# Loading k and q of the first two head pairs in long runs, with a repriced plan, in an attention and two-layer expert kernel

## The chip, the cores and the metric

One core of one Trainium2 chip runs the whole program. The metric is device time in microseconds of one execution, the median of several runs.

## The reference

Three layers, all in float32 (cut to what is computed):

```python
scores = 30 * tanh(q @ k.T / sqrt(64) / 30)      # 4 batches x 12 heads, 448 x 448, head size 64
x = softmax(scores) @ v                          # joined to 1792 tokens x 768
h = ((x @ w1) * (x @ w2)) @ w3 @ w_out           # 768 -> 1024 -> 1024 -> 768
e = argmax(h @ w_gate + modality_bias[modality_id]); gate = softmax(...)[e]
out[token] = gate * (relu(h @ m1[e]) @ m2[e])    # 8 experts
```

The weights w1, w2, w3 and w_out arrive as 64-bit floats and are brought to 32 bits on the chip.

## The kernel before

**Stages.** The attention stage handles 24 pairs of heads one after the other and, beside them, converts the 64-bit weights (in pieces: `L289` loads a piece into `raw`, four or five operations at `L224` to `L244` narrow it) and folds w3 with w_out into one matrix (`L648` to `L650`). Then `phase_x12` multiplies batches 0 and 1 of x with w1 and w2, `phase_x2` with the folded matrix, both again for batches 2 and 3, and at the end come the expert tiles. In these products each number is split into a high and a low part of type float32r, and a product is three passes: high weight by high x (`L1000`), high weight by low x (`L1001`), low weight by high x (`L1002`).

**A pair in the attention stage.** `load_k` (`L437`) and `load_q` (`L441`) bring both heads of a pair into `k2` and `q2`, with the order position group, head, element in each partition: the two heads of one position group lie side by side, so the load moves runs of 64 elements, 256 bytes. `load_v` (`L447`) brings v on POOL's queue. `tr_k` and `tr_q` turn k and q on TensorE (`L460`, `L474`) into a bank of the kind `tr`, of which there are two; `k_out` and `q_out` copy them out as KT and QT (`L252` on ScalarE or `L254` on VectorE). Scores are made at `L487`, tanh and exp at `L492` to `L498` into tiles of the kind `th` (seven buffers), sums of the exps on VectorE (`L523` to `L527`) and TensorE (`L534`, copied out as `smt`), and pv at `L507`. At the beginning 30 transposes of the identity (`L750`) keep TensorE busy; they hold one of the two `tr` banks until the last is done.

**The order of the work** in the attention stage is not written by hand. The class `Schedule` holds tasks with an engine, a duration in ns, a key (about four per pair), dependencies, and buffers that they take and use. `run` picks, again and again, the task that can start first, the smaller key first among equals, and emits it; so each engine's queue has the order of the plan. A load has a price `dma` in ns, which the plan adds to one common transfer queue: the load is taken to land when that queue has reached it, plus 1,100 ns. A dependency written `(lk, 0)` counts from the issue of the load and not from its landing. The plan alone decides order; on the chip an instruction waits for the tiles that it reads and overwrites. After the plan's end the stages are emitted in program order.

**At the seam**, x of batch 0 is split at `L933` (high parts, ScalarE) and `L935` (low parts, VectorE) in three pieces of two of its six 128-row blocks.

Of the kernel before, what the change touches and what calls it, by code (L numbers as in the profile page):

```python
# [8 lines left out]
F32 = mybir.dt.float32  # L9
# [111 lines left out]
def attention_moe_moe_kernel(  # L121
# [37 lines left out]
    nc = tc.nc  # L159
    B, H, S, D = q.shape  # L160
# [3 lines left out]
    P = 128  # L164
    CP = 112
    NC = S // CP
    KD = DM // P
# [32 lines left out]
    at1 = tc.alloc_tile_pool(name="at1", bufs=2, side="right", reuse_waits="tile")  # L200
# [6 lines left out]
    mm = nc.tensor.matmul  # L207
# [55 lines left out]
    class Stream:  # L263
# [17 lines left out]
        def add(self, pieces):  # L281
            n = len(pieces)
            self.todo += [(p, i, n) for i, p in enumerate(pieces)]
# [128 lines left out]
    sel = at1.tile([P, D], F32, name="sel", tag="sel", bufs=1)  # L412
    nc.gpsimd.memset(sel, 1.0)

    raw_qkv = {}

    def rows_of(r):
        return slice(D * r, D * r + D)
# [5 lines left out]
    def keys(t, g):  # L424

        return t[:, 4 * D:S].rearrange("h (p c) d -> h p c d", c=3) if g else t[:, 0:4 * D].rearrange("h (p c) d -> h p c d", c=4)

    def heads(t, p):
        b, hp = divmod(p, H // 2)
        return t[b, 2 * hp:2 * hp + 2]  # L430

    def load_k(p):
        k2 = at2.tile([P, NC, 2, D], F32, name="k2", tag="k2")
        q2 = at2.tile([CP, NC, 2, D], F32, name="q2", tag="q2")
        raw_qkv[p] = (k2, q2)
        for g in range(2):
            nc.sync.dma_start(k2[rows_of(g), 0:NC - g], keys(heads(k, p), g).rearrange("h p c d -> p c h d"))  # L437

    def load_q(p):
        eng = nc.sync if p else nc.scalar  # L440
        eng.dma_start(raw_qkv[p][1], heads(q, p).rearrange("h (p c) d -> p c h d", c=NC))  # L441

    def load_v(p):
        vt[p] = at1.tile([P, NC + NB, D], F32, name="vt", tag="vt", bufs=NV)
# [297 lines left out]
    add = sch.add  # L742

    def do(fn, *args):
        return lambda: fn(*args)
# [3 lines left out]
    for c in range(30):  # L749
        add("PE", 175, 1e6, lambda: nc.tensor.transpose(warm[:, 0:P], ident, ident),  # L750
            take=[("tr", "warm")] if c == 0 else [], use=[("tr", "warm")])
# [28 lines left out]
    for c in range(NW):  # L780
        u = c // 2
        key = (4.0 * c + 3) if c < 8 else (10 + 10.0 * c)
        raw, y, un = ("wraw", c), ("y", c), ("unit", u)
# [8 lines left out]
        if c < 8:  # L792
# [3 lines left out]
            for j in range(2):  # L796
                x = add("PE", 320, kg, do(tr_wo, c, j), [cn3[-1], *gate[-1:], *cps[-1:]], take=[tt[j], *([] if j else [("th", "o", c)])], use=[tt[j], y, ("th", "o", c)])
# [23 lines left out]
    for p in range(NP + 1):  # L821
        raw, vk, kt, qt = ("raw", p), ("v", p), ("KT", p), ("QT", p)
        hk, hq, sk, pk = ("tr", "k", p), ("tr", "q", p), ("sums", p), ("pv", p - 1)
        dep, use, take = [], [], []
        if p:
            dep, take, use = [ex[3], lv], [pk], [pk, ("th3", p - 1), ("v", p - 1)]
        if p < NP:
            k0, kk = 4 * p - 7, 4 * p - 4.0
            lk = add("SP", 1260, k0, do(load_k, p), take=[raw], use=[raw], dma=640)
            lq = add("SP" if p else "ACT", 630, k0 + 0.1, do(load_q, p), [(lk, 0)] if p else [], use=[raw], dma=640)  # L830
            lv = add("POOL", 2800, k0 + 4.0, do(load_v, p), [(lk, 0)], take=[vk], use=[vk], dma=640)
            t = add("PE", 380, 4 * p - 5.2, do(tr_k, p), [lk], take=[hk], use=[hk, raw])
            kl = add({'DVE': (620, 0), 'ACT': (530, 300)}, 0, kk, lambda eng, p=p: k_out(p, eng), [t], take=[kt], use=[hk, kt])
            t = add("PE", 380, 4 * p - 5.2, do(tr_q, p), [lq], take=[hq], use=[hq, raw])
            last_at2.append(t)
            ql = add({'DVE': (620, 0), 'ACT': (530, 300)}, 0, kk, lambda eng, p=p: q_out(p, eng), [t], take=[qt], use=[hq, qt])
            dep, take, use = dep + [kl, ql], take + [("sc", p, 3)], use + [("sc", p, 3), kt, qt]
        joint = add("PE", 770, 4 * p, do(pv_score, p), dep, take=take, use=use, mode="tiles")
        if p:

            for c in range(3):
                vl[p - 1, c] = add("PE", 770, 4 * p + c + 2.4, do(pv, p - 1, c), [ex[c], joint, vl.get((p - 1, c - 1))],
                                   use=[pk, ("th", p - 1, c), ("v", p - 1)], mode="tiles")
            smk = ("sc", "s", p - 1)
            sm = add("PE", 770, 4 * p + 2.9, do(sum_mm, p - 1), [ad], take=[smk], use=[smk, ("sums", p - 1)], mode="tiles")
            t = add({'ACT': (910, 0), 'DVE': (1090, 0)}, 0, 4 * p - 1, lambda eng, p=p: sum_out(p - 1, eng), [sm], take=[("smt", p - 1)], use=[smk, ("smt", p - 1)])
            ss = add("SP", 1260, 4 * p, do(sum_store, p - 1), [t], use=[("smt", p - 1)], dma=25)
            t = add("ACT", 530, 4 * p - 2, do(pv_copy, p - 1), [vl[p - 1, 2]], take=[("pvs", p - 1)], use=[pk, ("pvs", p - 1)])
            po[p - 1] = add("DVE", 620, 4 * p - 2, do(pv_out, p - 1), [t], use=[pk, ("pvs", p - 1)])
            st[p - 1] = add("SP", 630, 4 * p, do(pair_store, p - 1), [po[p - 1]], use=[("pvs", p - 1)], dma=640)  # L850
            last_at1 += [sm, ss] if p > NP - 2 else []
            b, r = divmod(p - 1, H // 2)
            if r == H // 2 - 1 and b < B - 1:
                t = add("SP", 630, 4 * p, lambda b=b: rs_t.__setitem__(b, sums_in(b)), [ss], dma=100)
                t = add("DVE", 500, 4 * p, lambda b=b: sums_add(rs_t[b]), [t])
                last_at2.append(add("SP", 630, 4 * p, lambda b=b: sums_out(b, rs_t[b]), [t], dma=100))
        if p == NP:
            break
        ex, ad = {}, None
        for n, c in enumerate(ORD):  # L860
            sc, th, i = ("sc", p, c), ("th3" if c == 3 else "th", p) + (() if c == 3 else (c,)), 4 * p + n
            if c < 3:
                t = add("PE", 770, i, do(score, p, c), [joint], take=[sc], use=[sc, kt, qt], mode="tiles")
            else:
                t = joint
            t = add("ACT", 600 if c == 3 else 950, i + 0.2, do(p_tanh, p, c), [t, cap_in], take=[th], use=[sc, th])
            ex[c] = add("ACT", 580 if c == 3 else 950, i + 1.1, do(p_exp, p, c), [t], use=[th])
        for c in (1, 2, 3):
            ad = add("DVE", 660 if c == 3 else 1120, 4 * p + 0, do(psum, p, c), [ex[c], *([ex[0]] if c == 1 else []), ad],
                     take=[sk] if c == 1 else [], use=[sk, ("th3", p) if c == 3 else ("th", p, c), *([("th", p, 0)] if c == 1 else [])])  # L870
# [24 lines left out]
    for n, (f, g) in enumerate(SWEEP):  # L895
        key = 5.4 * (n + 2) + 3
        raw, r_, h_, w_ = ("w3raw", n), ("w3r", n), ("tr", "w", n), ("w3t", n)
# [10 lines left out]
        for half in range(2):  # L908
# [3 lines left out]
                       take=[] if half else [fo], use=[fo, w_, ("unit", 2 * g), ("unit", 2 * g + 1)])  # L912
# [75 lines left out]
    def phase_x12(half, bs, hooks):  # L988
        gt = gp.tile([P, 2, KF, HALF], F32R, name="gT", tag="gT")
        units = {}  # L990
        for i, (u, j) in enumerate(ORDER[half]):
            if u not in units:
                units[u] = (ws.take(), ws.take())
            x = xt[bs[j]]
            for w, (wh, wl) in enumerate(units[u]):
                acc = acc2()
                for ft in range(2):
                    for d in range(KD):
                        o = d * 256 + ft * P
                        mm(acc[:, ft, :S], lhsT=wh[:, o:o + P], rhs=x[:, 0, d, :], start=(d == 0), stop=False)  # L1000
                        mm(acc[:, ft, :S], lhsT=wh[:, o:o + P], rhs=x[:, 1, d, :], start=False, stop=False)  # L1001
                        mm(acc[:, ft, :S], lhsT=wl[:, o:o + P], rhs=x[:, 0, d, :], start=False, stop=(d == KD - 1))  # L1002
                if w == 0:
                    a = wide("a").rearrange("p (f s) -> p f s", f=2)
                    nc.scalar.copy(a, acc[:, :, :S])
                else:
                    nc.vector.tensor_tensor(out=a, in0=acc[:, :, :S], in1=a, op=ALU.mult)
                    fs, sl = slice(2 * u, 2 * u + 2), slice(j * S, j * S + S)
                    nc.vector.tensor_copy(gt[:, 0, fs, sl], a)  # L1009
                    nc.gpsimd.tensor_tensor(out=gt[:, 1, fs, sl], in0=a, in1=gt[:, 0, fs, sl], op=ALU.subtract)  # L1010
                if u in [v for v, _ in ORDER[half][:i]]:
                    ws.free()
                ws.tick(nc.scalar, nc.vector)
                if (i, w) in hooks:
                    hooks[i, w]()
        return gt
# [332 lines left out]
```

## Time and profile before

| what | value |
|---|---|
| runs shown | 958.78, 961.33, 965.59 us; median 961.33 |
| the profiled execution | 963.59 us, span 961.7 us, mean granted TensorE clock 0.989 |
| TensorE busy | 924.1 us of the span |
| VectorE, ScalarE, POOL busy | 469.1, 374.9, 241.0 us |
| transfers | 132.73 MB, 138 GB/s over the span |

The span runs from the first to the last instruction. PE is TensorE and PEld its weight loads, DVE is VectorE, ACT is ScalarE; SPq and ACTq are the queues on which SyncE and ScalarE issue transfers. [...] Busy matmuls overlap, so a busy TensorE can still be slower than it could be.

### The profile page before, as it was taken

What the parts mean: (1) busy time and instruction counts of PE and PEld (TensorE: products, weight loads), DVE (VectorE), ACT (ScalarE), POOL (GpSimd) and SP (SyncE); (2) the same over time, 40 slices, a digit from 0 to 9 for tenths busy, and PEclk for the clock granted to TensorE, in tenths of its full rate; (3) what the DMA queues carried; (4) which work ended last, traced back from release to release, by engine and by line L of the source; (5) the groups of instructions that cost most, each with busy time, mean ns of one, the idle gap of its engine ahead of it and who ended that gap; (6) DMA issues with size and microseconds to landing.
All of it is one profiled execution on the core that took longest, in us unless ns stands there. A gap on an engine that the chain in (4) does not pass through costs nothing. (4 is left out here: it accounts for less than half of the span.)

```text
span 961.7 us, 13900 instructions
## 1 busy us (share of the span) xinstructions
PE 924.1 (96%) x5618; PEld 763.5 (79%) x5618; DVE 469.1 (49%) x671; ACT 374.9 (39%) x447; POOL 241.0 (25%) x211
## 2 busy tenths in 40 slices
PE   8999989999999999999999999999999999999994
PEld 5456555655655799999999999999899899889894
DVE  4999986786675478721006422100653523423410
ACT  4897766776775333231222211211422312322400
POOL 3434211151110112123542441200604212302011
PEclk9899999999999999999999999999999999999998
DMA  9767785477544565626622341310671591782401
GB/s 225 206 167 219 203 243 141 129 217 179 156 140 121 146 193 164 186 79 215 171 93 96 78 120 34 115 50 33 166 178 43 184 172 33 199 148 52 160 20 44
DMA packets 126088, 132.73 MB, mean 138 GB/s; under 512 B 60926, under 2 KB 107416, under 8 KB 126021
## 3 DMA queue, kind: packets, MB, share of 16 engines
q1 hardware_dynamic: 112644, 114.35, 42.3%
q0 software_dynamic: 12464, 17.22, 7.9%
q8 instruction: 46, 0.75, 0.3%
q10 hardware_dynamic: 912, 0.23, 0.1%
q14 instruction: 22, 0.17, 0.1%
HBM read 102.13 MB, written 30.19 MB: 138 GB/s over the span
## 5 line engine op out<-in xcount | busy, mean ns | idle before, releaser
L1001 PE MATMUL acc<-xT,wh 128*128 128x448 f32 x384 | 141.4, 368 | 0.7 <-DVE xT L935 0.7
L1000 PE MATMUL acc<-xT,wh 128*128 128x448 f32 x384 | 140.4, 366 | 1.5 <-ACT xT L933 1.5
L1002 PE MATMUL acc<-xT,wl 128*128 128x448 f32 x384 | 140.4, 366 | 0.0
L329 DVE TENSOR_TENSOR wl<-raw,wh 128x1536 fp32r<-128x1536 f32 (+1 forms) x42 | 73.6, 1759 | 116.8 <-ACT wh L252 116.8
L252 ACT CAST wh<-raw 128x1536 fp32r<-128x1536 f32 (+1 forms) x48 | 70.3, 1479 | 105.4 <-DMA raw<-in_moe_w_dram 78.5
L487 PE MATMUL sc<-QT,KT 64*64 64x448 f32 x672 | 92.9, 561 | 7.9 <-ACT smt L252 4.2
L507 PE MATMUL pv<-th,vt 64*64 64x448 f32 x672 | 89.2, 551 | 0.0
L498 ACT ACTIVATE th<-th,capb 128x448 f32<-128x448 f32 (+1 forms) x96 | 89.0, 956 | 0.6
L1214 PE MATMUL acc<-wh,hT 128*124 128x384 f32 x256 | 87.8, 343 | 1.1 <-DVE y L1222 0.7
L447 POOL DMA_DIRECT2D vt<-in_v_dram x96 | 50.9, 545 | 146.3 <-PE pv L507 144.9
L1216 PE MATMUL acc<-wh,hT 128*124 128x384 f32 x256 | 86.5, 338 | 0.7 <-DVE hT L1185 0.7
L1215 PE MATMUL acc<-wl,hT 128*124 128x384 f32 x256 | 86.3, 337 | 0.5 <-DVE wl L329 0.5
L1010 POOL TENSOR_TENSOR gT<-a,gT 128x896 fp32r<-128x896 f32 x16 | 43.8, 2740 | 144.2 <-DVE gT L1009 138.7
L1000 PEld LDWEIGHTS acc<-xT,wh 128*128 128x128 f32 x384 | 72.5, 189 | 8.2 <-ACT xT L933 2.3
L1001 PEld LDWEIGHTS acc<-xT,wh 128*128 128x128 f32 x384 | 72.6, 189 | 7.0 <-DVE xT L935 1.2
L492 ACT ACTIVATE th<-sc,icap 128x896 f32<-128x896 f32 x72 | 71.2, 1010 | 16.2 <-PE sc L487 15.6
L1002 PEld LDWEIGHTS acc<-xT,wl 128*128 128x128 f32 x384 | 72.6, 189 | 5.3
L1032 PE MATMUL acc<-wh,gT 128*128 128x388 f32 x224 | 76.4, 341 | 0.0
L1033 PE MATMUL acc<-wl,gT 128*128 128x388 f32 x224 | 76.0, 339 | 0.0
L1034 PE MATMUL acc<-wh,gT 128*128 128x388 f32 x224 | 75.9, 339 | 0.0
L1180 PE MATMUL acc<-xsT,wh 128*128 128x496 f32 x192 | 74.9, 390 | 0.0
L1182 PE MATMUL acc<-xsT,wl 128*128 128x496 f32 x192 | 74.5, 388 | 0.0
(163 smaller groups left out, 1630.1 us busy)
## 6 DMA issues: line engine op xcount, KB each, us to landing
raw<-in_moe_w_dram SPq DMA_DIRECT2D x48, 768.0 KB
w3raw<-in_moe_w_dram SPq DMA_DIRECT2D x16, 512.0 KB
raw<-w_scr SPq DMA_DIRECT2D x8, 776.0 KB
raw<-in_moe_w_out_dram SPq DMA_DIRECT2D x8, 768.0 KB
w_scr<-y SPq DMA_DIRECT2D x16, 384.0 KB
raw<-w_scr SPq DMA_DIRECT2D x8, 768.0 KB
x_scr<-pvs SPq DMA_DIRECT2D x24, 224.0 KB
xraw<-x_scr SPq DMA_DIRECT2D x4, 1344.0 KB
```

The lines of the kernel that those rows point to most:

```text
L487: mm(sc[rows_of(side(p, j, g)), g, :S], lhsT=KT[p][rows_of(j), o:o + D], rhs=QT[p][rows_of(j), :], start=True, stop=True)
L498: nc.scalar.activation(tht[p, c], tht[p, c], ACTF.Exp, scale=capb)
L507: mm(pvb[p][rows_of(j), r, :S], lhsT=vt[p][rows_of(r), NC * g + c, :], rhs=tht[p, c][rows_of(r), g, :] if c < NB else tht[p, c][rows_of(r) ...
L1000: mm(acc[:, ft, :S], lhsT=wh[:, o:o + P], rhs=x[:, 0, d, :], start=(d == 0), stop=False)
L1001: mm(acc[:, ft, :S], lhsT=wh[:, o:o + P], rhs=x[:, 1, d, :], start=False, stop=False)
L1002: mm(acc[:, ft, :S], lhsT=wl[:, o:o + P], rhs=x[:, 0, d, :], start=False, stop=(d == KD - 1))
L1032: mm(acc[:, hf, :HA], lhsT=gt[:, 0, f, ts], rhs=wh[:, o:o + HA], start=(f == 0), stop=False)
L1033: mm(acc[:, hf, :HA], lhsT=gt[:, 0, f, ts], rhs=wl[:, o:o + HA], start=False, stop=False)
L1034: mm(acc[:, hf, :HA], lhsT=gt[:, 1, f, ts], rhs=wh[:, o:o + HA], start=False, stop=(f == KF - 1))
L1214: mm(acc[:TP, hf, :HT], lhsT=ht[:, 0, f, cs], rhs=wh[:, o:o + HT], start=(f == 0), stop=False)
L1215: mm(acc[:TP, hf, :HT], lhsT=ht[:, 0, f, cs], rhs=wl[:, o:o + HT], start=False, stop=False)
L1216: mm(acc[:TP, hf, :HT], lhsT=ht[:, 1, f, cs], rhs=wh[:, o:o + HT], start=False, stop=(f == KF - 1))
```

## The change

For the pairs 0 and 1 (`NF = 2`) k and q are loaded into a tile `run` with the order head, position group, element, in runs of 1,024 bytes (768 for the second half of k); two VectorE copies for k and one ScalarE copy for q then put them in the order that `tr_k` and `tr_q` read. The tiles are of the kind `th`. In the plan, v depends on the landing of k (for pairs 0 and 1 on the copy), no longer on k's issue; the price of a load of k or q goes from 640 to 700 for the first two pairs and to 2,300 for the others, that of v from 640 to 900. In `phase_x12` the passes with the high part of x come first for all six blocks, then those with the low part.

```diff
+    NF = 2
...
     def load_k(p):
...
+        if p < NF:
+            runs[p] = [at1.tile([P, 2, NC, D], F32, name="run", tag="th", bufs=7) for _ in range(2)]
         for g in range(2):
-            nc.sync.dma_start(k2[rows_of(g), 0:NC - g], keys(heads(k, p), g).rearrange("h p c d -> p c h d"))
+            n, src = NC - g, keys(heads(k, p), g)
+            if p < NF:
+                nc.sync.dma_start(runs[p][0][rows_of(g), :, 0:n], src.rearrange("h p c d -> p h c d"))
+            else:
+                nc.sync.dma_start(k2[rows_of(g), 0:n], src.rearrange("h p c d -> p c h d"))
 
     def load_q(p):
...
+            eng = nc.sync if p else nc.scalar
+            eng.dma_start(runs[p][1][0:CP], src.rearrange("h (p c) d -> p h c d", c=NC))
...
+    def order_k(p):
+        for g in range(2):
+            n = NC - g
+            nc.vector.tensor_copy(raw_qkv[p][0][rows_of(g), 0:n], runs[p][0][rows_of(g), :, 0:n].rearrange("p h c d -> p c h d"))
+
+    def order_q(p):
+        nc.scalar.copy(raw_qkv[p][1], runs[p][1][0:CP].rearrange("p h c d -> p c h d"))
...
-            lk = add("SP", 1260, k0, do(load_k, p), take=[raw], use=[raw], dma=640)
-            lq = add("SP" if p else "ACT", 630, k0 + 0.1, do(load_q, p), [(lk, 0)] if p else [], use=[raw], dma=640)
-            lv = add("POOL", 2800, k0 + 4.0, do(load_v, p), [(lk, 0)], take=[vk], use=[vk], dma=640)
+            first = p < NF
+            rk, rq = [("th", "run", p, i) for i in range(2)] if first else [None] * 2
+            lk = add("SP", 1260, k0, do(load_k, p), take=[raw, rk, rq] if first else [raw], use=[raw, rk] if first else [raw], dma=700 if first else 2300)
+            lq = add("SP" if p else "ACT", 630, k0 + 0.1, do(load_q, p), [(lk, 0)] if p else [], use=[raw, rq] if first else [raw], dma=700 if first else 2300)
+            if first:
+                lk = add("DVE", 1050, kk, do(order_k, p), [lk], use=[raw, rk])
+                lq = add("ACT", 620, kk, do(order_q, p), [lq], use=[raw, rq])
             t = add("PE", 380, 4 * p - 5.2, do(tr_k, p), [lk], take=[hk], use=[hk, raw])
...
+            lv = add("POOL", 2500, k0 + 4.0, do(load_v, p), [lk], take=[vk], use=[vk], dma=900)
...
                 for ft in range(2):
-                    for d in range(KD):
-                        o = d * 256 + ft * P
-                        mm(acc[:, ft, :S], lhsT=wh[:, o:o + P], rhs=x[:, 0, d, :], start=(d == 0), stop=False)
-                        mm(acc[:, ft, :S], lhsT=wh[:, o:o + P], rhs=x[:, 1, d, :], start=False, stop=False)
-                        mm(acc[:, ft, :S], lhsT=wl[:, o:o + P], rhs=x[:, 0, d, :], start=False, stop=(d == KD - 1))
+
+                    for part in range(2):
+                        for d in range(KD):
+                            o = d * 256 + ft * P
+                            mm(acc[:, ft, :S], lhsT=wh[:, o:o + P], rhs=x[:, part, d, :], start=(d == part == 0), stop=(part == 1 and d == KD - 1))
+                            if part == 0:
+                                mm(acc[:, ft, :S], lhsT=wl[:, o:o + P], rhs=x[:, 0, d, :], start=False, stop=False)
```

## Rows read from the trace of the kernel before

**Rows 1.** The page: the span, and each engine's busy time, share and instructions.

```profile
span 961.7 us, 13900 instructions
...
PE 924.1 (96%) x5618; PEld 763.5 (79%) x5618; DVE 469.1 (49%) x671; ACT 374.9 (39%) x447; POOL 241.0 (25%) x211
```

**Rows 2.** Windows of the span: length, busy us by engine, granted clock, DMA share, GB/s.

```profile
0.00:20.00 20.00, 15.27 (x90) 9.97 (x90) 5.82 (x14) 6.75 (x9) 7.04 (x18) 1.00 1.02 212
20.00:315.00 295.00, 278.22 (x2264) 165.19 (x2260) 230.98 (x354) 218.31 (x289) 73.73 (x109) 0.98 0.64 178
40.00:60.00 20.00, 19.30 (x165) 9.74 (x169) 19.73 (x30) 18.55 (x27) 7.21 (x7) 0.91 0.67 180
320.00:340.00 20.00, 20.00 (x99) 18.31 (x99) 7.53 (x8) 4.04 (x5) 6.39 (x3) 1.00 0.59 153
```

**Rows 3.** Timeline of the first 30 us: start, length, engine, line, idle before and releaser.

```profile
0.87 1.68 SPq L437 DMA_DIRECT2D k<-in_k_dram  x2
...
1.57 4.43 POOL L447 DMA_DIRECT2D vt<-in_v_dram  x8 [0.25 <-issue]
...
7.24 1.17 PE L460 MATMUL tr<-ident,k 128*128 128x128 f32 x4 [2.46 <-DMA k<-in_k_dram]
...
8.34 3.67 PE L750 MATMUL tr<-ident 128*128 128x128 f32 x16
...
8.45 0.62 DVE L254 COPY KT<-tr 128x448 f32<-128x448 f32 x1 [0.17 <-PE tr L460]
...
11.81 0.95 PE L474 MATMUL tr<-ident,q 112*128 112x112 f32 x4
...
14.01 2.69 PE L487 MATMUL sc<-QT,KT 64*64 64x448 f32 x20
...
15.25 0.56 DVE L234 TENSOR_SCALAR y<-y 128x768 f32<-128x768 f32 x1
...
18.23 0.59 PE L507 MATMUL pv<-th,vt 64*64 64x448 f32 x2
```

**Rows 4.** Windows of 1 us, columns as in rows 2.

```profile
11.00:12.00 1.00, 1.00 (x7) 1.00 (x6) 0.00 (x0) 0.00 (x0) 0.00 (x0) 1.00 1.04 371
...
19.00:20.00 1.00, 1.00 (x12) 0.21 (x8) 0.00 (x0) 1.00 (x3) 0.00 (x0) 1.00 1.33 185
```

**Rows 5.** Timeline from 130 to 145 us.

```profile
130.05 1.85 SPq L437 DMA_DIRECT2D k<-in_k_dram  x2
...
136.62 0.43 SPq L289 DMA_DIRECT2D raw<-in_moe_w_dram  x1
...
141.93 0.89 ACT L224 ACTIVATE y<-raw 128x768 f32<-128x768 f32 x1 [3.61 <-DMA raw<-in_moe_w_dram]
...
143.65 0.89 ACT L252 COPY smt<-sc 128x896 f32<-128x896 f32 x1
...
144.59 0.59 PE L487 MATMUL sc<-QT,KT 64*64 64x448 f32 x2 [3.15 <-ACT smt L252]
```

**Rows 6.** Windows of 2 us, columns as in rows 2.

```profile
146.00:148.00 2.00, 2.00 (x16) 1.12 (x12) 2.00 (x5) 1.85 (x3) 0.00 (x0) 0.50 0.01 2
...
316.00:318.00 2.00, 1.67 (x5) 1.49 (x6) 2.00 (x3) 0.83 (x1) 0.00 (x0) 0.64 0.93 240
318.00:320.00 2.00, 2.00 (x7) 1.79 (x6) 0.28 (x1) 0.00 (x0) 0.00 (x0) 0.51 0.97 352
```

**Rows 7.** Timeline from 314 to 317 us.

```profile
314.21 2.62 ACT L933 CAST xT<-xraw 128x896 fp32r<-128x896 f32 x3
...
315.19 3.10 DVE L935 TENSOR_TENSOR xT<-xraw,xT 128x896 fp32r<-128x896 f32 x3 [0.21 <-ACT xT L933]
...
315.21 0.47 PE L1000 MATMUL acc<-xT,wh 128*128 128x448 f32 x1 [1.48 <-ACT xT L933]
...
316.33 0.58 PE L1001 MATMUL acc<-xT,wh 128*128 128x448 f32 x1 [0.66 <-DVE xT L935]
```

More of the change, by code (lines that the diff above doesn't have):

```diff
@@ L413, in attention_moe_moe_kernel @@
     nc.gpsimd.memset(sel, 1.0)
-    raw_qkv = {}
+    raw_qkv, runs = {}, {}
+    NF = 2
     def rows_of(r):
@@ L435, in load_k @@
         raw_qkv[p] = (k2, q2)
+        if p < NF:
+            runs[p] = [at1.tile([P, 2, NC, D], F32, name="run", tag="th", bufs=7) for _ in range(2)]
         for g in range(2):
-            nc.sync.dma_start(k2[rows_of(g), 0:NC - g], keys(heads(k, p), g).rearrange("h p c d -> p c h d"))
-    def load_q(p):
-        eng = nc.sync if p else nc.scalar
-        eng.dma_start(raw_qkv[p][1], heads(q, p).rearrange("h (p c) d -> p c h d", c=NC))
+            n, src = NC - g, keys(heads(k, p), g)
[3 more added lines that the diff above has]
+                nc.sync.dma_start(k2[rows_of(g), 0:n], src.rearrange("h p c d -> p c h d"))
+    def load_q(p):
+        src = heads(q, p)
+        if p < NF:
+            eng = nc.sync if p else nc.scalar
+            eng.dma_start(runs[p][1][0:CP], src.rearrange("h (p c) d -> p h c d", c=NC))
+        else:
+            nc.sync.dma_start(raw_qkv[p][1], src.rearrange("h (p c) d -> p c h d", c=NC))
+    def order_k(p):
[4 more added lines that the diff above has]
+        nc.scalar.copy(raw_qkv[p][1], runs[p][1][0:CP].rearrange("p h c d -> p c h d"))
     def load_v(p):
```

## The prediction

> **What bounds the kernel now.** The page comes first: TensorE is busy for 924.1 of 961.7 us, the other engines for half or less [rows 1]. Whatever the change does must show as TensorE time, so the second view is the busy time by stretches [rows 2]: in the fused products from 320 us on, TensorE works 20.00 of 20 us; in the first 20 us it works 15.27; and between 20 and 315 us, the attention stage, it is idle for 295 - 278.22 = 16.8 us, with a mean granted clock of 0.98, which is about another 0.02 x 295 = 5.9 us lost. So the time to be won is some 4.7 us at the start, some 22 us spread over the attention stage, and the seam to the products. Within the attention stage TensorE is not alone: from 40 to 60 us VectorE is busy for 19.73 and ScalarE for 18.55 of 20 us [rows 2], and an instruction that waits in one of these queues costs at once.
>
> **The start, before.** The third view is the order of time [rows 3]. k of pair 0 is issued at 0.87 us; TensorE waits 2.46 us for it and turns it at 7.24. The last 16 of the 30 warm-up transposes follow (3.67 us, 0.229 each), q is turned only at 11.81, because its bank is the warm-up's, and the first scores stand at 14.01. Two single microseconds of the transfer show the price of short runs [rows 4]: 185 GB/s while 256-byte runs of k and q dominate, 371 GB/s while the long runs of the weights do.
>
> **The start, after.** One load of k or q is 2 x 448 x 64 x 4 = 0.229 MB, so k and q of one pair are 0.459 MB: 2.48 us at 185 GB/s, 1.24 us at 371. Runs of 1,024 and 768 bytes lie between; k of pair 0 lands between 0 and 1.24 us earlier. I take 1.0, since these runs are nearer to the long ones: 6.24 instead of 7.24. New on the path is putting k in order, two copies of 512 and 384 columns. By the copy out of PSUM (448 columns, 0.62 us) that is 1.24 us, by the operation on SBUF alone (768 columns, 0.56 us) it is 0.65 [rows 3]; with the handoff I take 1.1. So k is turned at 7.34, no earlier than before. What moves is the warm-up: the planner charges 1,050 ns plus a lag of 160 for the ordering and 175 per warm-up transpose, so about 7 more of them go ahead of k and 9 instead of 16 stand behind it. From turning k to turning q went 4.57 us; it becomes 4.57 - 7 x 0.229 = 2.97, q at 10.3, and the first scores at about 12.5. **Term: -1.5 us**, with ends of -2.1 (all of the 1.24, the cheap copy) and +0.5 (no gain in the transfer, the dear copy, and the second pair's ordering standing ahead of q's copy on VectorE). [...]
>
> The ordering of both q's on ScalarE (at most 0.89 us each, the price of a copy of 896 columns [rows 5]) and of the second k on VectorE lies beside the warm-up; VectorE has only the first KT copy there [rows 3]. Without that cover each would cost its 0.6 to 1.1 us. The four run tiles take four of the seven th buffers; pair 0's tanh uses the other three, and the four are free again before pair 1's.
>
> **v waits for k** only in the plan. The planner before already made v depend on the issue of k, yet v of pair 0 goes out at 1.57 us, while k's issue lasts until 0.87 + 1.68 = 2.55 [rows 3]: a dependency of the plan places an instruction in its queue and is no wait on the chip. On POOL's queue v of pairs 0 to 2 stays first, so nothing is queued behind it that was not before. Term: 0. If a real wait did appear, v would come later by up to some 5 us; its first reader, pv of pair 0 at 18.23, comes 4.2 us after the first scores [rows 3], so the cost would be up to some 1 us.
>
> **Dearer loads.** The planner charged 640 ns for a load of k or q, and charges 2,300 for pairs 2 to 23; by 185 GB/s a load takes 1.24 us. Both are wrong, one by half, the other by almost twice, but they err on opposite sides. What too cheap a load does shows at 130 to 145 us [rows 5]: loads of k and q go out from 130.05 on, a weight piece at 136.62, and ScalarE stands in front of its first operation on that piece for 3.61 us until 141.93. Queued behind it is the copy of the sums, 143.65, which frees the bank that the scores need; TensorE sits 3.15 us, and from 146 to 148 us the granted clock is 0.50, the lower of its two levels [rows 6]. At half speed those 2 us alone lose 1.0; the two records at the seam (0.64 and 0.51 over 2 us each, so 0.72 + 0.98) put the loss of one such stretch at 1.7 us. With 1,660 ns more on each of the two loads ahead, the plan expects the piece 3.3 us later, close to the 3.61 by which it was wrong, and would put other work of ScalarE ahead of it. **Term: -3.15 - 1.7 = -4.85 us.** Its ends are 0 (the order is new everywhere, and another stall takes its place) and, by the rivals below, more on either side. What is late next there is the sum copy itself, behind one exp.
>
> **x12's passes.** ScalarE splits x in three pieces (2.62 us from 314.21), VectorE makes the low parts (3.10 us from 315.19); TensorE starts at 315.21 after 1.48 us, does one pass and waits another 0.66 us for the first low part [rows 7]. After the change the first 12 passes need high parts alone. The second piece of high parts is due at about 314.21 + 2 x 0.87 = 315.95, the third at 316.83, and passes 5 and 9 want them at 316.0 and 316.8 at the earliest (20 us hold 99 passes, 0.2 each [rows 2]); the low parts come one by one until 318.3, and passes 13 to 18 want them from 317.6 to 318.6. So the 0.66 us goes and the 1.48 stays. The number of passes and weight loads is the same, and in the full stretch the passes already run without a gap [rows 2], so nothing else moves. **Term: -0.66 us.** The clock falls there too (0.64, then 0.51 [rows 6]), about 1.7 us; whether a single shorter gap still brings it down no row tells, so I leave it in and keep -1.7 as the other end.
>
> **The sum.** -1.5 - 4.85 - 0.66 = -7.0 us. The profiled execution took 963.6 us (961.7 of it the span): 956.6. That execution is 2.3 us above the median of the runs shown, 961.3; from the median the same sum gives 954.3, and I keep 956.6, because part of the stall may well return in another place.
>
> **Rivals.**
> 1. *The planner trades stall for stall.* All of the attention stage is planned anew. The stall at 141.9 goes, another in-order wait of a like size comes. Only the start and the seam remain: 963.6 - 2.2 = 961.4. For it: the stage has 16.8 us of idle time in many small pieces, of which the 3.15 is one.
> 2. *The dearer loads mend more than this one place.* Loads that land when the plan says also spare it other waits. A third of what the stage still loses, (16.8 + 5.9 - 4.85) / 3 = 6.0 us, would go too: 950.6. Against it: the rows show one stall of this kind, and the rest of the idle time is in small pieces that a transfer need not have caused.
> 3. *Slower: k and q are turned too late.* The plan charges 2 x 2.3 = 4.6 us for a pair where the rows give 2.48; 2.1 us too much each pair, while transfers already fill 0.67 of the time between 40 and 60 us [rows 2]. In pairs 2 to 9 the planned queue would run up to 8 x 2.1 = 17 us behind, and the turning of k is placed behind products that need not come first. Half of that, 8.5, and one more stretch at the lower clock, 1.7, would cost 10.2: 963.6 - 2.2 + 10.2 = 971.6. It decides once the planned backlog passes one pair's time, (315 - 14) / 24 = 12.5 us, as a pair is loaded about one pair ahead. Against it: VectorE, at 19.73 of 20, is the slower resource there, and keeps its order of work mostly.
> 4. *The change does nothing of the kind*: the runs are not faster and v goes out as before. Then the ordering costs what the warm-up gives back, and the time is that of rival 1.
>
> **Chances.** The forecast 0.38 (its own range 952 to 961), rivals 1 and 4 together 0.19, rival 2 0.30, rival 3 0.13. About 1%, 9.6 us, is what a measurement can tell from no change: faster means below 951.7, slower above 970.9. Faster: 0.22 of rival 2 and 0.04 from the forecast's low end, 0.26. Slower: 0.10 of rival 3. The rest, 0.64, is within 1%. The range runs from 946 (rival 2 with the clock's 1.7 us at the seam and some more of the stage) to 967 (rival 1 with half of rival 3), and leaves out some 2 in 10.
>
> **What would show it.** The start: the wait for k ends near 6.2 us and 9 warm-up passes follow the turning of k; the first scores stand near 12.5. v of pair 0 still issued at about 1.6. The stall: no wait of ScalarE over 3 us for a weight piece, and TensorE idle below 13 us between the start and the seam. The seam: one gap of about 1.5 us and none for VectorE. Wrong would be: TensorE waiting for turned k in pairs 2 to 9 (rival 3), a new wait of 3 us elsewhere (rival 1), or first scores at 14 us or later.

## The result, and the profile after

The changed kernel took 950.7 us (median of 4 runs) where the kernel before took 963.5 in the same comparison (4 runs): a ratio of 0.9864, interval 0.9822 to 0.9906. The two profiled executions took 947.1 and 963.6 us.

The page of the changed kernel, its span and busy times (answers to [rows 1]):

```profile
span 945.2 us, 13904 instructions
...
PE 914.5 (97%) x5618; PEld 756.4 (80%) x5618; DVE 472.8 (50%) x677; ACT 375.9 (40%) x447; POOL 238.2 (25%) x211
```

The number of matmuls is the same, 5,618. The span splits at four moments that one reads from the timeline: first scores, the seam (first pass of x12), first pass of x2, first expert pass.

| stretch | before | after | difference |
|---|---|---|---|
| to the first scores | 14.01 | 11.04 | -2.97 |
| first scores to seam | 301.20 | 291.68 | -9.52 |
| x12, first half | 119.39 | 118.67 | -0.72 |
| x2 to first expert pass | 238.41 | 238.14 | -0.27 |
| experts to the end | 288.69 | 285.66 | -3.03 |

The last line is no work of the change: the program there is the same, and over the 14 profiled executions of this study it took 285.6 to 291.3 us. That is part of why the profiled pair differs by 16.5 us and the medians by 12.7.

Windows of the stage from first scores to seam, before and after (columns as in rows 2):

```profile
14.01:315.21 301.20, 283.59 (x2306) 166.52 (x2305) 234.75 (x362) 223.46 (x295) 73.73 (x109) 0.98 0.65 180
```

```profile
0.00:20.00 20.00, 16.23 (x117) 9.15 (x117) 10.46 (x22) 10.89 (x14) 7.14 (x18) 1.00 0.99 218
11.04:302.72 291.68, 278.95 (x2306) 162.70 (x2305) 236.71 (x364) 222.93 (x293) 72.79 (x109) 0.99 0.69 187
```

TensorE's idle time in the stage falls from 301.20 - 283.59 = 17.6 us to 12.7, which is 4.9 of the 9.5 us. Most of the rest goes with the clock: the mean grant rises from 0.98 to 0.99, some 3 us. The grant is a share of full speed; in windows of 0.5 us over either whole trace it reads 1.00 or 0.50, and values between only in windows at the edges of a stretch at 0.50. Behind the seam of before TensorE starts a pass of x12 every 0.37 us at 0.50 (317.09 to 319.33 us) and every 0.20 to 0.21 us at 1.00 (320.03 to 320.85). Before, it is at 0.50 three times in the stage, from about 30, 43 and 146 us; after, once, from about 57 us (two windows of before, the third is in [rows 6]; then the one of after):

```profile
29.90:33.20 3.30, 3.30 (x20) 1.25 (x22) 3.27 (x7) 2.34 (x4) 0.00 (x0) 0.50 0.47 104
43.50:46.80 3.30, 3.30 (x20) 1.18 (x24) 3.27 (x6) 2.25 (x5) 2.31 (x1) 0.50 0.64 206
```

```profile
56.60:59.90 3.30, 3.30 (x20) 1.34 (x22) 3.27 (x8) 1.99 (x3) 0.00 (x0) 0.50 1.10 274
```

ScalarE's longest wait for a weight piece in the stage is 0.63 us, where before it was 3.61 [rows 5]:

```profile
130.75 0.94 ACT L224 ACTIVATE y<-raw 128x768 f32<-128x768 f32 x1 [0.63 <-DMA raw<-in_moe_w_dram]
```

The start of the changed kernel, in order of time (answers to [rows 3]; L457 puts k in order, L769 is the warm-up):

```profile
0.87 1.42 SPq L442 DMA_DIRECT2D run<-in_k_dram  x2
...
1.57 6.74 POOL L466 DMA_DIRECT2D vt<-in_v_dram  x12 [0.24 <-issue]
...
4.55 0.42 DVE L457 COPY k<-run 64x512 f32<-64x512 f32 x1 [2.79 <-DMA run<-in_k_dram]
...
6.55 0.55 DVE L457 COPY k<-run 64x384 f32<-64x384 f32 x1 [1.59 <-DMA run<-in_k_dram]
...
7.16 0.75 PE L479 MATMUL tr<-ident,k 128*128 128x128 f32 x4 [1.26 <-DVE k L457]
...
7.84 1.20 PE L769 MATMUL tr<-ident 128*128 128x128 f32 x9
...
8.88 0.55 PE L493 MATMUL tr<-ident,q 112*128 112x112 f32 x4
...
11.04 2.69 PE L506 MATMUL sc<-QT,KT 64*64 64x448 f32 x20
```

k is turned at 7.16 us, hardly earlier than the 7.24 of before. What got shorter comes after: 9 warm-up passes in 1.20 us, 0.133 each, where before 16 took 0.229 each.

The seam of the changed kernel (answers to [rows 7]; L1026 uses the high weights, L1028 the low ones, L957 makes high parts):

```profile
301.73 2.62 ACT L957 CAST xT<-xraw 128x896 fp32r<-128x896 f32 x3
...
302.72 0.47 PE L1026 MATMUL acc<-xT,wh 128*128 128x448 f32 x1 [1.49 <-ACT xT L957]
303.03 0.36 PE L1028 MATMUL acc<-xT,wl 128*128 128x448 f32 x1
...
317.56 1.78 ACT L957 CAST xT<-xraw 128x896 fp32r<-128x896 f32 x2 [13.21 <-DVE xraw L963]
...
319.39 0.47 PE L1026 MATMUL acc<-xT,wh 128*128 128x448 f32 x1 [1.81 <-ACT xT L957]
```

The gap of 0.66 us is gone. Further on stands a new one of 1.81 us: batch 1 is not yet split when TensorE comes to it.

### The profile page after: what moved, and what is told of

Its sections match the earlier page's. It is cut to its first block, busy times and chain, and to the rows that moved or that the text cites. A ratio compares the mean times of both kernels' runs of the same rounds, so it can differ in the third digit from the quotient of the medians.

```text
span 945.2 us, 13904 instructions
## 1 busy us (share of the span) xinstructions
PE 914.5 (97%) x5618; PEld 756.4 (80%) x5618; DVE 472.8 (50%) x677; ACT 375.9 (40%) x447; POOL 238.2 (25%) x211
## 5 line engine op out<-in xcount | busy, mean ns | idle before, releaser
L1026 PE MATMUL acc<-xT,wh 128*128 128x448 f32 x768 | 218.5, 365 | 3.3 <-ACT xT L957 3.3
L1026 PEld LDWEIGHTS acc<-xT,wh 128*128 128x128 f32 x768 | 144.2, 188 | 15.7 <-ACT xT L957 4.4
L1028 PE MATMUL acc<-xT,wl 128*128 128x448 f32 x384 | 139.7, 364 | 0.0
L329 DVE TENSOR_TENSOR wl<-raw,wh 128x1536 fp32r<-128x1536 f32 (+1 forms) x42 | 73.6, 1759 | 117.5 <-ACT wh L252 117.5
L506 PE MATMUL sc<-QT,KT 64*64 64x448 f32 x672 | 87.7, 551 | 4.2 <-DVE wst L676 1.5
L526 PE MATMUL pv<-th,vt 64*64 64x448 f32 x672 | 85.9, 543 | 1.2 <-DVE pvs L569 1.2
L1028 PEld LDWEIGHTS acc<-xT,wl 128*128 128x128 f32 x384 | 72.1, 188 | 5.4
L1206 PE MATMUL acc<-xsT,wh 128*128 128x496 f32 x192 | 74.9, 390 | 0.0
L1207 PE MATMUL acc<-xsT,wh 128*128 128x496 f32 x192 | 73.8, 384 | 0.0
L506 PEld LDWEIGHTS sc<-QT,KT 64*64 64x64 f32 x672 | 25.7, 133 | 42.5 <-issue 16.1
```

What stands on the lines that cost most here:

```text
L506: mm(sc[rows_of(side(p, j, g)), g, :S], lhsT=KT[p][rows_of(j), o:o + D], rhs=QT[p][rows_of(j), :], start=True, stop=True)
L526: mm(pvb[p][rows_of(j), r, :S], lhsT=vt[p][rows_of(r), NC * g + c, :], rhs=tht[p, c][rows_of(r), g, :] if c < NB else tht[p, c][rows_of(r) ...
L1026: mm(acc[:, ft, :S], lhsT=wh[:, o:o + P], rhs=x[:, part, d, :], start=(d == part == 0), stop=(part == 1 and d == KD - 1))
L1206: mm(acc[:, ft, :T], lhsT=wh[:, o:o + P], rhs=xt[:, 0, d, :], start=(d == 0), stop=False)
```

## The experiments

Two theories stood against each other on the stage from first scores to seam. **A**: time is lost where the queue of ScalarE or VectorE stands in front of a weight piece that has not landed; a plan with dearer transfers puts other work there. **B**: a new plan is a draw, some microseconds either way. "Waits for pieces" below is the sum of the idle times just ahead of the first operation on a loaded piece (L224, L226, starting from 16 to 312 us) that the trace puts down to a transfer or to "issue". VectorE's waits for the first pieces lie before 16 us: counted from the first scores on, the changed kernel has 2.9 us and the kernel before still 7.1. Ratios are to the kernel before, in the runs of the same comparison.

| kernel | ns for k, q | ns for a piece | v | long runs | waits for pieces, us | scores to seam, us | ratio |
|---|---|---|---|---|---|---|---|
| before | 640 | 2,185 | old | no | 7.1 | 301.2 | 1 |
| e1, only x12 | 640 | 2,185 | old | no | 7.3 | 301.7 | 0.9969 |
| e2, only runs | 640 | 2,185 | old | yes | 9.3 | 301.7 | 0.9980 |
| e3, only price | 2,300 | 2,185 | old | no | 0.2 | 294.5 | 0.9914 |
| e4, only v | 640 | 2,185 | new | no | 2.9 | 296.2 | 0.9933 |
| e9, only pieces' price | 640 | 3,845 | old | no | 3.4 | 295.8 | 0.9910 |
| after | 2,300 | 2,185 | new | yes | 0.6 | 291.7 | 0.9864 |
| e5, old x12 | 2,300 | 2,185 | new | yes | 0.2 | 291.6 | 0.9854 |
| e6, old v | 2,300 | 2,185 | old | yes | 8.9 | 299.2 | 0.9858 |
| e7 | 640 | 2,185 | new | yes | 8.8 | 296.9 | 0.9924 |
| e8 | 1,240 | 2,185 | new | yes | 9.0 | 301.4 | 0.9932 |
| e10 | 2,300 | 1,100 | new | yes | 5.0 | 306.1 | 0.9986 |
| e11 | 2,200 | 2,185 | new | yes | 3.8 | 292.9 | 0.9874 |

Two profiles of the same plan (before and e1; after and e5) agree within 0.5 us in the stage. A profile is still one draw: the four runs of the changed kernel go from 947.1 us (mean granted clock 0.994) to 960.5 (0.984).

**e1, only the passes of x12** (on the kernel before):

```diff
-                    for d in range(KD):
...
+                    for part in range(2):
+                        for d in range(KD):
```

> The kernel before with the reordered passes of x12 alone. My theory: the 0.66 us wait for the first low part at the seam goes, and with one gap fewer the clock does not fall there, so 0.7 + 1.7 = 2.4 us less than before, some 961 us where before has 963.5. Rival (the clock falls there anyway): 0.7 us less, and windows of 2 us behind the seam still at about 0.5.

Measured: 0.9969, interval 0.9949 to 0.9989, 3 us less. The wait at the seam is gone and the clock does not fall there; windows of e1 behind the seam, to be set against 0.64 and 0.51 in [rows 6]:

```profile
316.00:318.00 2.00, 2.00 (x12) 1.63 (x11) 2.00 (x3) 0.96 (x2) 0.00 (x0) 1.00 0.94 215
318.00:320.00 2.00, 2.00 (x12) 1.87 (x11) 0.41 (x1) 0.00 (x0) 0.00 (x0) 1.00 1.02 356
```

The first half of x12 took 117.5 instead of 119.4 us. My theory holds on this plan.

**e2, only the long runs and the ordering** (x12, v and the later prices as before; first pairs 700):

```diff
+            runs[p] = [at1.tile([P, 2, NC, D], F32, name="run", tag="th", bufs=7) for _ in range(2)]
...
+    def order_k(p):
```

> The kernel before with the long runs and the ordering for pairs 0 and 1 alone; all prices of later loads, v's dependency and x12 as before. Theory A (the start is carried to the end): first scores at about 11.0 us instead of 14.0, total 3 us less, about 960.5. Theory B (the planner's new order matters more than the start): first scores at 11.0 all the same, but the attention stage behind it differs by several us either way.

Measured: 0.9980, 0.9956 to 1.0005. First scores at 9.95 us, 4 us earlier than before. VectorE now waits 2.74 and ScalarE 2.50 and 3.39 us for pieces, but the stage behind the start is no longer than before (301.7 against 301.2 us), so this profile carries the earlier start to the seam. In the timed runs the total moves by some 2 us, and the interval goes from 4 us less to 0.5 more: whether the start is carried to the end (theory A, 3 us) stays open.

**e3, only the price of k and q**:

```diff
-take=[raw], use=[raw], dma=640)
+take=[raw], use=[raw], dma=2300 if p > 1 else 640)
```

> The kernel before with the price of a load of k and q at 2,300 ns for pairs 2 to 23 alone. Theory A (dearer loads mend waits of ScalarE and VectorE for weight pieces): the two waits of ScalarE for a weight piece, 6.7 us in all, are gone or below 1 us, and the attention stage from first scores to seam, 301 us before, is 5 to 9 us shorter; about 956. Theory B (a plan is a draw, prices do not steer it): the stage differs by up to 5 us either way, with waits for pieces still there.

Measured: 0.9914, 0.9882 to 0.9947. Both waits are gone, the stage is 6.7 us shorter, as A has it: TensorE's idle time in it falls from 17.6 to 12.5 us, and the mean grant rises from 0.98 to 0.99.

**e4, only v's dependency and prices**:

```diff
-            lv = add("POOL", 2800, k0 + 4.0, do(load_v, p), [(lk, 0)], take=[vk], use=[vk], dma=640)
+            lv = add("POOL", 2500, k0 + 4.0, do(load_v, p), [lk], take=[vk], use=[vk], dma=900)
```

> The kernel before with v's new dependency and price (900 ns, 2,500 ns to issue) alone. My theory: v of pair 0 is issued at 1.6 us as before, since the dependency is no wait on the chip; the stage stays within 2 us of before, about 963. Theory B (a plan is a draw): up to 5 us either way though nothing on the chip waits longer for v. Rival (v really waits): v of pair 0 issued after 7 us.

Measured: 0.9933, 0.9913 to 0.9953. v of pair 0 is issued at 1.57 us here, as in every kernel of the study but one (1.56), so it waits for nothing on the chip. Yet the stage is 5.0 us shorter. My "within 2 us" was wrong: the price of v enters the same planned queue as the pieces, and the waits for pieces fall to 2.9 us. Whether it is the price or the new place of v in the plan was not tried apart.

**e5, the changed kernel with x12's old passes** (the diff of e1 backwards):

> The changed kernel with x12's passes in the old order. My theory: the wait of 0.66 us for the first low part is back at the seam and the clock falls there again, 2.4 us more than the changed kernel (ratio to before about 0.989 where the changed kernel has 0.9864). Rival (nothing but the one wait): 0.7 us more.

Measured: 0.9854, 0.9815 to 0.9893, no loss that the runs can tell. The gap of 0.66 us came back, as expected, and a second one of 1.55 us is batch 1's; but the clock stayed up (1.00 from 302 to 330 us), so the larger part of the expected 2.4 us is missing:

```profile
304.07 0.47 PE L1025 MATMUL acc<-xT,wh 128*128 128x448 f32 x1 [0.66 <-DVE xT L959]
...
320.53 0.47 PE L1025 MATMUL acc<-xT,wh 128*128 128x448 f32 x1 [1.55 <-DVE xT L959]
```

In x12 alone e5 took 119.5 us and the changed kernel 118.7. So the reorder is worth 1.9 us on the old plan (e1) and 0.8 on the new one, where the wait for batch 1 follows it.

**e6, the changed kernel with v as before** (the diff of e4 backwards):

> The changed kernel with v's dependency and price as before. My theory: v is issued at the same moment at the start, and the time is within 3 us of the changed kernel (ratio 0.984 to 0.990). Theory B (a plan is a draw): the attention stage differs by up to 5 us.

Measured: 0.9858, 0.9819 to 0.9898, no loss that the runs can tell. Its profile does not say the same: the stage took 299.2 us with 8.9 us of waits for pieces, the whole 951.9 against 945.2. Part of this is the draw of the profiles: that of e6 is the slowest of its four runs (953.9 us, median 952.8), that of the changed kernel its fastest (947.1, median 950.7). What stays is that e6 has as many waits for pieces as e7 and e8 below and no loss in time that its runs can tell. That speaks against A in its plain form, in which each such wait is paid for, and no run settles it.

**e7 and e8, the changed kernel with 640 and 1,240 ns for k and q**:

```diff
-dma=700 if first else 2300)
+dma=700 if first else 640)
```

> The changed kernel with the price of k and q at 640 ns again for pairs 2 to 23. Theory A (dearer loads mend in-order waits): the waits of ScalarE for weight pieces return, 5 us or more in all, and the stage from first scores to seam is 5 to 9 us longer than the changed kernel's 291.7: ratio about 0.993 to 0.996. Theory B (a draw): any ratio from 0.98 to 0.995 without more of those waits.

Measured for e7: 0.9924, 0.9893 to 0.9955; the waits are back at 8.8 us, the stage is 5.2 us longer. That fits A. Another 3.1 us are lost in x12, where TensorE waits 3.33 us for batch 1 (1.81 in the changed kernel): the prices also move the moment at which batch 1's x is ready.

> The changed kernel with 1,240 ns, the price that 185 GB/s gives, for k and q of pairs 2 to 23. Theory A': what counts is that the price is true, so 1,240 does as well as 2,300 or better, ratio 0.986 or below. Theory A'': only a price that is too high keeps loads out of the way, so 1,240 lies half way, ratio about 0.990. Theory B (a draw): no order between 640, 1,240 and 2,300.

Measured for e8: 0.9932, 0.9897 to 0.9967. The price that the measured rate gives is no better than 640, so it is not the true price of k and q that counts (A' falls), nor is there an order in the price. But what happens in e8 is the stall of before over again:

```profile
134.22 0.53 SPq L289 DMA_DIRECT2D raw<-in_moe_w_dram  x1
...
140.72 0.89 ACT L224 ACTIVATE y<-raw 128x768 f32<-128x768 f32 x1 [4.81 <-issue]
...
142.44 0.89 ACT L252 COPY smt<-sc 128x896 f32<-128x896 f32 x1
...
143.39 1.01 PE L506 MATMUL sc<-QT,KT 64*64 64x448 f32 x2 [4.35 <-ACT smt L252]
```

A piece goes out at 134.22, ScalarE stands 4.81 us in front of it (the trace says "issue", but the operation reads the piece), the copy of the sums comes behind it, and TensorE is idle for 4.35 us.

**e9, the kernel before with a dearer weight piece**, k, q and v as they were:

```diff
-        t = add("SP", 630, key - 2, ws.load1, take=[raw], use=[raw], dma=2185, deps=[ld])
+        t = add("SP", 630, key - 2, ws.load1, take=[raw], use=[raw], dma=3845, deps=[ld])
```

> The kernel before with the plan's price of a weight piece at 3,845 ns instead of 2,185 (1,660 more, as the change adds to a load of k or q) and nothing else. Theory A (the time is lost in ScalarE and VectorE queues that stand in front of a piece that has not landed): these waits, 7.1 us before, fall below 1 us though k and q keep their cheap price, and first scores to seam goes from 301.2 to 291 to 296 us, ratio 0.985 to 0.992. Theory B (a plan is a draw): the stage anywhere from 291 to 306, not tied to the waits. Theory C (it is the price of k and q itself, which places their turning): the stage stays near 301.

Measured: 0.9910, 0.9877 to 0.9943; the stage 295.8 us; waits for pieces 3.4 us, more than the 1 expected. With k and q at their old price the gain of e3 is there, which theory C excludes. But only 2.6 of the 5.4 us are TensorE's idle time (15.0 instead of 17.6); the rest goes with the clock, which does not fall once in this stage (1.00 instead of 0.98).

**e10, the changed kernel with a cheaper weight piece** (`dma=1100`):

> The changed kernel with the price of a weight piece at 1,100 ns instead of 2,185, the price of k and q left at 2,300. Theory A: waits of 4 us or more in all for pieces return and the stage from first scores to seam grows from 291.7 to 296 or more, ratio to before 0.990 or above. Theory B: no tie between the two. Theory C: the stage stays near 292.

Measured: 0.9986, 0.9951 to 1.0021: the whole gain is lost by one number. ScalarE waits again:

```profile
85.36 0.90 ACT L224 ACTIVATE y<-raw 128x768 f32<-128x768 f32 x1 [2.91 <-DMA raw<-in_moe_w_out_dram]
...
90.38 0.89 PE L506 MATMUL sc<-QT,KT 64*64 64x448 f32 x2 [3.26 <-DVE wst L676]
...
131.28 0.92 ACT L224 ACTIVATE y<-raw 128x768 f32<-128x768 f32 x1 [2.11 <-DMA raw<-in_moe_w_dram]
```

The stage, 306.1 us, is longer than the 5.0 us of waits alone explain. The mean granted clock in it is 0.97 where the changed kernel has 0.99, and this profile is one of the two slowest of ten runs. x12 took 4.0 us more than in the changed kernel, with a wait of 4.41 us for batch 1.

**e11, the changed kernel with 2,200 ns** as a control:

> The changed kernel with 2,200 ns instead of 2,300 for k and q of pairs 2 to 23: a control for how much a plan of nearly the same prices differs. Theory A: waits for pieces stay below 1 us and the stage from first scores to seam is 289 to 295. Theory B (a draw): it may be at 297 to 302 with no cause to name.

Measured: 0.9874, 0.9810 to 0.9937; the stage 292.9 us, waits 3.8 us. Nearly the same prices give nearly the same time, though not the waits below 1 us that I expected. B in its strong form, in which any price may give any time, is not borne out; it is one control.

**e12, the changed kernel with another order of units in x12's first half**:

```diff
-        [(0, 0), (0, 1), (1, 0), (1, 1), (2, 0), (2, 1), (3, 1), (3, 0)],
+        [(0, 0), (1, 0), (0, 1), (1, 1), (2, 0), (2, 1), (3, 1), (3, 0)],
```

> The changed kernel with one more edit: x12's first half multiplies batch 0 with weight units 0 and 1 before it turns to batch 1, whose x the changed kernel waits 1.8 us for at 317.6. Theory: that wait goes, the x12 stage falls from 118.7 to about 117.0 us, and the total is 1.7 us below the changed kernel, ratio about 0.9845. Rival: the second unit's weights are late instead, and TensorE waits about as long for them.

Measured: 0.9951, 0.9923 to 0.9978, 8 us or so more than the changed kernel. The rival came true and was dearer than the cure:

```profile
330.12 0.89 ACT L224 ACTIVATE y<-raw 128x768 f32<-128x768 f32 x1 [7.08 <-DMA raw<-in_moe_w_dram]
...
335.11 0.74 PE L1026 MATMUL acc<-xT,wh 128*128 128x448 f32 x1 [9.52 <-ACT wh L252]
```

In the changed kernel batch 1's passes with unit 0 stand there, from 319.39 us on, and cover the loading of unit 1, whose pieces go out at 323.31. Now nothing covers it, and the wait stands in the open for 9.5 us. No kernel of the study beats the changed one clearly.

## Why the prediction was right, and where it was not

The direction and the range held, and the main mechanism fits all runs but e6; the size, 956.6 against 950.7 us, was that of rival 2 (950.6). That this number is met so closely is in part luck: of the 16.5 us between the two profiles 3.0 lie in the expert stage, where the program is the same, and the start gave twice its term.

**The start: right in k by luck, mis-sized behind it.** k was to be turned at 7.34 and was at 7.16, but by two errors that cancel. Its second half landed at some 6.5 us instead of 6.24, since from 4 to 6 us, with v's loads beside it, the transfers move far less than the 371 GB/s that I leaned on (columns as in rows 2, GB/s last):

```profile
4.00:5.00 1.00, 1.00 (x7) 1.00 (x5) 0.42 (x1) 0.62 (x1) 1.00 (x2) 1.00 0.74 165
5.00:6.00 1.00, 0.90 (x6) 0.66 (x5) 0.00 (x0) 0.00 (x0) 1.00 (x3) 1.00 1.17 176
```

The ordering costs 0.6 us on the path and not 1.1, because its first copy (0.42) runs before the second half lands. Over all profiles k is turned at 6.57 to 7.28 us with short runs (five kernels) and at 6.39 to 7.26 with long ones (nine).

The nine warm-up passes stand where I put them. But I priced them at the 0.229 us of before, and they ran at 0.133. The term was -2.97, not -1.5. I read the 0.229 as the rate of the lower clock. The column of the granted clock does not show it, as it reads 1.00 in every window of the start before and after; but e3 turns a k in a stretch that is granted 0.50, and its four passes take 1.12 us, as they do at the start of before (1.17) and not as in the changed kernel (0.75):

```profile
101.55 1.12 PE L460 MATMUL tr<-ident,k 128*128 128x128 f32 x4 [1.95 <-DVE w3l L627]
```

```profile
101.70:103.70 2.00, 2.00 (x7) 1.55 (x7) 2.00 (x6) 0.53 (x1) 1.17 (x2) 0.50 0.42 112
```

In all nine kernels with 21 warm-up passes in one stretch ahead of k, the nine behind k took 1.20 us. With 14 ahead and then the gap of 1.8 to 2.5 us, four of five kernels kept the slow rate for the next 16 (3.67 or 3.68 us), and one, e9, did not (1.97 us):

```profile
1.53 3.25 PE L750 MATMUL tr<-ident 128*128 128x128 f32 x14 [1.53 <-DVE ident L217]
...
7.23 1.97 PE L750 MATMUL tr<-ident 128*128 128x128 f32 x16
...
9.04 0.55 PE L474 MATMUL tr<-ident,q 112*128 112x112 f32 x4
...
11.53 2.69 PE L487 MATMUL sc<-QT,KT 64*64 64x448 f32 x20
```

There the old start, with short runs, has its first scores at 11.53, within 0.5 us of the changed kernel and inside the 9.95 to 12.34 of the nine kernels with long runs. So most of the start's gain is the quicker rate, which comes earlier and which I read as that of the upper clock; of the long runs themselves little is left, since the ordering eats what the transfer saves. That the longer stretch of warm-up work causes the earlier change of rate was not tried by itself, and e9 shows that the old stretch can have it too.

**v: right on the chip, open in the sum.** It waits for nothing (issued at 1.57). But I set its term to 0 by looking at POOL's queue alone. Its price moves the planned landing of everything behind it, and on the old plan e4 gains 0.5 to 0.9% by v's edit. On the new plan, taking that edit back loses nothing that the runs can tell (e6), so what v gave to the changed kernel stays open.

**Dearer loads: right mechanism, half its size.** The stall at 141.9 us and its loss of clock went, and e8 shows the same chain when it returns. I counted that one place, 4.85 us; the price alone gained 6.7 in the stage (e3) and the whole change 9.5. The plan also spared ScalarE the wait of 3.04 us at 125 and other, smaller ones, and the two falls of the clock at 30 and 43 us went, with one new at 57; how the rest divides between them no run shows. I called both prices of k and q wrong, on opposite sides, and chose the dear side from one piece, which it moved by about the right 3.3 us. It is not a matter of the true price: the truer 1,240 did no better than 640 (e8), and dearer pieces alone (e9) did as well as dearer k and q alone (e3). The account that fits most runs is that a queue that the plan holds to be longer than it is keeps first uses away from landings, whichever price makes it longer. e6 does not fit it.

**x12: right, and partly eaten.** The 0.66 us went, and the 1.7 us of clock that I kept as the other end went too (e1). Of the six kernels with the old passes four lose the clock within 2.5 us behind the seam (e2, e3, e9 and before, with 0.50 from 317.0 to 319.5 us) and two keep it (e4, and e5 with 1.00 from 302 to 330 us); of the eight with the new passes none loses it there (the changed kernel: 1.00 from 302 to 310 us). On the new plan a wait of 1.81 us for batch 1 came in their place, which I did not name.

**The rivals.** The turning of k and q (rival 3) did not become late: TensorE's longest gap in the stage is 1.6 us, and it waits for a QT copy. Stall for stall (rival 1) is what e8 and e10 are; the change did not meet it.

## What to carry to other kernels

In a planned schedule with in-order queues, compare each first use of a loaded tile with its landing in the trace: where the use stands early, what is queued behind it can pay, also on engines that never read the tile (in e8 ScalarE stood 4.81 us in front of a piece and TensorE was idle for 4.35). In this kernel it paid to err on the late side in the price of transfers (nothing above 2,300 and 3,845 ns was tried). Then profile the plan and time it several times, since no rule found here says beforehand that 1,240 ns is too little. Here a gap that was closed uncovered the next one (batch 1, 1.81 us in the changed kernel; unit 1, 9.52 us in e12): look at what it covered before removing it.

## What the runs showed of the hardware that was not expected

The two copies that put k in order took 0.42 us for 512 columns and 0.55 us for 384, in the rows of the start above: the smaller one is slower, and so it is in all nine kernels that have the pair (0.42 to 0.48 against 0.55 us). They differ in their outer size, 4 against 3, and in the partitions that they use; which of the two counts was not tried. The ordering of k thus takes 0.97 us in all, and the part with fewer columns is the dearer one.
